# Attention heads beside an H3 convolution on one core: named jobs run from one list, PSUM as four pairs of banks

## The chip, the core and the metric

The kernel runs on one core of a Trainium2 chip. The metric is the device time of one execution in microseconds (us): the median of three runs. A profiled execution of the same program gives a trace, whose span runs from the first to the last instruction.

TensorE (PE in the profile) multiplies matrices and writes its results to PSUM, which is eight banks of 128 partitions x 512 float32 here. ScalarE (ACT) moves results from PSUM to the on-chip memory (an "evacuation" below) and makes exponentials, logarithms and sines. VectorE (DVE) makes the elementwise products and sums. GpSimd (POOL) and SyncE (SP) issue most of the DMA transfers. Each engine runs its own instructions in the order in which the program lists them; semaphores make one engine wait for another.

## What is computed

Two independent parts, both on a sequence of S = 2048 rows of D = 576, their outputs side by side in one array of 2048 x 1152 in bfloat16:

```python
# A: attention, 32 heads of 18; a row sees itself and 7 rows before it, 2 apart
qkv = x @ wqkv
logits[h, s, w] = (q[h, s] . k[h, s - 2w]) * 18 ** -0.5      # w = 0..7, masked where s - 2w < 0
a = (sum over w of softmax(logits)[h, s, w] * v[h, s - 2w]) @ wo
# B: H3
kv = (4-tap causal filter of k along the sequence, by shift_k) * v
y  = causal convolution of kv with ssm_k (length 2048), by FFT, + kv * ssm_D
b  = q * y
out = concat([a, b], -1)
```

## The kernel before

All weights and activations stay on the chip; the sequence is cut into two halves for A (1024 rows each) and four blocks of 512 rows for B. The work has these stages, with the lines of the kernel before:

- **Projection** (`project`, matmuls L363 and L367, tails L374 and L380, evacuation L397): for each component, half and tile of 128 channels, four k-tiles of 128 rows by 512 columns, plus a "tail" of 64 rows for the fifth k-tile. A flag decides whether the tails come first or last in a group. `transpose_tail` (L469) makes the input of the tails. `table_i` (L432) makes tables of sines for the inverse transform by transposing on TensorE and copying on ScalarE.
- **Shift filter** (`taps`, L554 to L580) on VectorE: four taps and the product with v, for each of the four blocks.
- **Spectra.** `mirror` (L589, L592) folds a block of kv and `fold_filter` (L650, L653) a block of the filter; `filter_spectrum` (L610, L611, L670) and `x_spectrum` (L766, L768) multiply by tables of sines and cosines. Each of these units is small: four to eight matmuls into one pair of banks, then one or two evacuations. `turn_filter`, `third`, `first_rows` and `negate` are small copies and sums around them, some as accumulating DMAs from POOL's queue.
- **Logits** (`logits`): VectorE multiplies q by shifted k (L822), TensorE sums over the channels of a head by a matrix of ones and zeros (L837), ScalarE evacuates (L842). Two half-passes (hh = 0 and 1) of ten products each.
- **Softmax** (`softmax`, L855 to L882): maxima and differences on VectorE (L865 to L869), the exponential on ScalarE (L871), the sum on TensorE (L877), the reciprocal by logarithm and exponential on ScalarE (L878, L879), the scaling on VectorE (L882).
- **Weighted values.** `spread` (L917) copies the probabilities of 32 heads' rows over the channels by four DMAs on SP's queue (L925); `weigh` multiplies by shifted v on VectorE (L947) and adds up on TensorE (L964, L978); ScalarE evacuates (L968, L982). There are six spreads, numbered 0 to 5, three for each half-pass.
- **Output projection** (`output`, L1012, L1020, L1031, stores L1035) with the weight that POOL's queue loads (L995, L998).
- **Convolution.** For each block j of the output, third t of the frequencies and block i of the input: a product of spectra on VectorE (L1098) and a sum on TensorE (L1126, evacuated at L1139, the last one by VectorE at L1137). Some products need the sum of two of a spectrum's three parts first (L1247). Then `inverse` (L1146; L1158, L1177, evacuated at L1161 and L1179), `back` (L1193; L1199, L1185, evacuated at L1206), and the gate by q on VectorE (L1212; the last block's in pieces at L1167). `load_q` (L1085) brings a block of q on POOL's queue into one of two slots; `store_b` (L1077) stores a gated block from the same slot, on SP's queue and partly on ScalarE's.

**What sets the order.** The program is written out by Python when it is built. VectorE's chain of logits, softmax and weighted values is the backbone, and small units of TensorE work wait in a queue `units`. At 48 places of the backbone `until` (L333) takes as many units from the queue as a hand-written tuple `PLACES` says; each time the first unit whose "due" time on a planner's clock has come. `dve` (L312) and `pe` (L318) advance these clocks by estimated durations; `need` (L340) takes units until none of a given name is left. Further tuples (`FKS`, `FXS`, `EARLY`, `AT`) place units in the queue.

**PSUM.** The eight banks are four pairs. A pool with two buffers has two tags, A and B, each of two pairs. Which tag a unit uses is fixed by its kind: projections, mirrors, folds and, until the logits run, filter spectra use A; logits, softmax sums, weighted values and spectral sums use B. Three kinds of small units pick among A and B by a turn of their own:

```python
    def filler_tag(kind, tags):
        turns[kind] += 1
        return tags[turns[kind] % len(tags)]
    def bank2(name, tag):
        return pp.tile([128, 2, 512], FP32, name=name, tag=tag)
```

A new tile of a tag waits until the tile two before it of the same tag has been evacuated.

Of the kernel before, what the change touches and what calls it, by code (L numbers as in the profile page):

```python
# [12 lines left out]
ALU = mybir.AluOpType  # L13
# [5 lines left out]
PLACES = (  # L19
    15, 4, 11, 2, 1, 0, 3, 4, 6, 4, 13, 4, 4, 0, 4, 3, 4, 2, 1, 3, 4, 3, 5, 5, 0, 7, 2, 2, 2, 1, 2, 2, 2, 2, 3,  # L20
    1, 0, 3, 2, 0, 8, 3, 0, 1, 12, 1, 1, 0,
)

FKS = (
    3, 1, 0, 0, 0, 0, 0, 0, 0, 0, 0, 0, 0, 0, 0, 0, 0, 0, 1, 0, 0, 0, 0, 2, 0, 0, 2, 0, 0, 0,
)
FXS = (
    7, 2, 0, 12, 13, 2, 0, 0, 4,
)

EARLY = (
    0, 0, 4,
)

AT = (
    2, 10, 17,
)
# [8 lines left out]
def kernel(  # L46
# [48 lines left out]
    pp = ctx.enter_context(tc.tile_pool(name="pp", bufs=2, space=PSUM))  # L95

    turns = {"fk": 0, "fx": 0, "wo": 0}

    def filler_tag(kind, tags):

        turns[kind] += 1
        return tags[turns[kind] % len(tags)]

    def bank2(name, tag):
        return pp.tile([128, 2, 512], FP32, name=name, tag=tag)

# [41 lines left out]
    warm = sp1.tile([128, 1], FP32, name="warm")  # L152
# [7 lines left out]
    def idle_work(n):  # L160
        ps = bank2("ps_idle", "A")
        for _ in range(n):
            nc.tensor.matmul(ps[:, 0, :], zeros[:, 0:128], zeros, start=True, stop=True)

# [137 lines left out]
    v = None  # L302
# [3 lines left out]

    units = deque()
    tasks = deque()
    clk = {"D": 0.0, "P": 0.0, "A": 0.0}
    psum = {"A": deque([0.0, 0.0]), "B": deque([0.0, 0.0])}  # L310

    def dve(n, fn, ready=0.0, ns=0.53):  # L312

        fn()
        clk["D"] = max(clk["D"], ready) + n * ns / 1000 + 0.125
        return clk["D"]

    def pe(us, tag, evac, ready=0.0, first=True, last=True):  # L318

        clk["P"] = max(clk["P"], ready, psum[tag].popleft() if first else 0.0) + us  # L320
        clk["A"] = max(clk["A"], clk["P"] + 0.1) + evac
        if last:
            psum[tag].append(clk["A"])
        return clk["A"]

    def pop(n=0):
        f = units[n][1]
        del units[n]
        f()

    places = iter(PLACES)

    def until():  # L333

        for _ in range(next(places, 0)):
            if units:
                p = max(clk["P"], psum["A"][0] if psum["A"] else 0.0)
                pop(next((n for n, u in enumerate(units) if len(u) < 4 or u[3] <= p), 0))

    def need(label):  # L340
        while any(u[2] == label for u in units):
            pop()

    def due(slack=0.0):

        while tasks and tasks[0][0] <= clk["D"] + slack:
            tasks.popleft()[1]()
# [4 lines left out]
    def dest(comp, ct):  # L352
        if comp == 0:
            return q, (ct * S if ct < 4 else 4 * S), 0
        return (k if comp == 1 else v), (ct * KW if ct < 4 else 4 * KW), PAD


    def project(comp, jj):
# [24 lines left out]
        def unit(ct, jj, jp, first, box):  # L383
            t, o, pad = dest(comp, ct)
            if jp == 0:
                box["ps"] = bank2("ps_proj", "A")
                if first:
                    tails(box["ps"], ct, jj, True)
            ps = box["ps"]
            body(ps, ct, jj, jp, first)  # L390
            if jp == 0:
                clk["P"] += 1.15 if first else 0.9
                return
            if not first:
                tails(ps, ct, jj, False)
            pe(0.9 if first else 1.15, "A", 1.02)
            nc.scalar.activation(view(t, o + pad + 1024 * jj, [[512, 2], [1, 512]]), ps[:], ACT.Copy)  # L397
            if ct == 4 and comp > 0:
                (nc.gpsimd if comp == 1 else nc.sync).dma_start(view(t, o, [[1, PAD]])[64:128, :], view(t, o + 1024, [[1, PAD]])[0:64, :])

        for ct in range(4) if jj < 2 else [4]:
            first = ct % 2 == 1 if ct < 4 else comp == 1
            box = {}
            for jp in range(2):
                units.append((0.9 + 0.25 * (jp != first), partial(unit, ct, jj % 2, jp, first, box),
                              f"v{jj}{ct}" if comp == 2 else f"proj{comp}"))
# [25 lines left out]
    def table_i(s):  # L432

        ps = bank2("ps_ti", "A")
# [6 lines left out]
        for g2 in range(2):  # L441
            nc.scalar.activation(view(TI, 1024 * s + 512 * g2, [[256, 2], [4, 64], [1, 4]]),
                                 view(ps, 512 * g2, [[256, 2], [1, 64], [64, 4]]), ACT.Copy)

# [17 lines left out]
    def pair_x():  # L462
        return pp.tile([128, 2, 1024], BF16, name="ps_x", tag="B")

    def early(f, us):
        f()
        clk["P"] += us

    def transpose_tail(jj):  # L469
        pt = pp.tile([128, 512], FP32, name="ps_x", tag="B")  # L470
# [4 lines left out]
        nc.scalar.activation(x5(jj), pt[:], ACT.Copy)  # L475

    def project_first(jp, ct0):

        ps = bank2("ps_proj", "A")
# [7 lines left out]
        nc.scalar.activation(view(q, S * ct0 + 512 * jp, [[S, 2], [1, 512]]), ps[:], ACT.Copy)  # L487

    def spread_taps(n0):
        n = min(256, D - n0)  # L490
        ps = bank2("ps_sk", "A" if n == 256 else "B")
        for h in range(0, n, 128):
            w = min(128, n - h)
            sk = skrow[:, 4 * (n0 + h):4 * (n0 + h + w)].rearrange("p (d j) -> p d j", j=4)
            for r in range(2):
# [4 lines left out]
                             ps[:].rearrange("p b (d j) -> p j (b d)", j=4)[:, :, 0:n], ACT.Copy)  # L500

# [3 lines left out]
    pts = [pair_x() for _ in range(2)]  # L505
# [6 lines left out]
    copy_tail(0, pts[1])  # L512
    spread_taps(256)
    sines += [table_x(0), table_x(1)]
    project_first(0, 0)
    pts = [pair_x() for _ in range(2)]
# [5 lines left out]
    copy_tail(1, pts[0])  # L522
    project_first(0, 2)
# [4 lines left out]
    for jj in range(2):  # L528
        if jj:
            project(0, jj)  # L530
# [773 lines left out]
```

## Time and profile before

| | |
|---|---|
| three runs | 213.05, 213.20, 213.38 us |
| median | 213.2 us |
| span of the profiled execution | 211.5 us |
| mean granted TensorE clock | 0.998 |
| busy: TensorE, VectorE | 200.9 and 197.3 us |
| busy: ScalarE, GpSimd | 151.0 and 69.3 us |
| moved by DMA | 36.12 MB, mean 171 GB/s |

In the rows below, a windows row has the stretch, its length, then for each engine (PE, PEld for weight loads, DVE, ACT, POOL) its busy time with the number of instructions, then the granted clock, the DMA share and GB/s. A waits row has the engine, the output and line that waited, the releaser it waited for, the total, the number of times and the longest, in us. A timeline row has the start, the length of the run of like instructions, the engine, the line, the operation with output and input, the number of them, and in brackets the idle time before it with what ended it. SPq is the issue of a DMA on SP's queue. A row of a group of instructions has their busy time and mean in ns, and then the idle time before them. A row of DMA issues ends in the median time from issue to landing.

### The profile page before, as it was taken

Reading aid. Unit: us, or ns where it says so; the run is one execution under the profiler, and the core shown is the slowest. Engines: PE = TensorE matmul, PEld = TensorE weight load, DVE = VectorE, ACT = ScalarE, POOL = GpSimd, SP = SyncE. Lnnn points to the kernel's source line nnn. Section 1 sums busy time; section 2 is a strip of 40 time slices with the busy share of each in tenths; the row PEclk is TensorE's granted clock in tenths of the full one; section 3 lists DMA queues with packets and bytes.
Section 4 is the critical chain, followed back from the end, with each engine's and each line's share of the span. In section 5 each row is a group of like instructions: output and inputs, shape, how many; then the busy total and the mean of one; then the engine's idle time right before and its main releaser. Section 6 shows DMA issues by size and latency. Waiting matters only on the chain.

```text
span 211.5 us, 5096 instructions
## 1 busy us (share of the span) xinstructions
PE 200.9 (95%) x2122; PEld 112.5 (53%) x2122; DVE 197.3 (93%) x150; ACT 151.0 (71%) x218; POOL 69.3 (33%) x104
## 2 busy tenths in 40 slices
PE   7999899999879999999999999999999999999891
PEld 2543344445545556563345566765567667676560
DVE  7989999999978999979979999999999999899982
ACT  3799766967797989984378688864487896765640
POOL 8999991023391367220090000004240000202000
PEclk9999999999999999999999999999999999999999
DMA  6999999999092636998999896589993105453034
GB/s 204 297 317 239 248 323 322 183 238 286 8 135 33 87 56 105 187 159 187 226 222 228 141 232 154 103 211 249 209 278 107 60 3 160 123 167 115 3 106 117
DMA packets 34084, 36.12 MB, mean 171 GB/s; under 512 B 17459, under 2 KB 28847, under 8 KB 34062
## 3 DMA queue, kind: packets, MB, share of 16 engines
q1 hardware_dynamic: 26380, 23.11, 43.8%
q0 software_dynamic: 5216, 10.19, 24.8%
q10 hardware_dynamic: 2466, 2.51, 3.6%
q8 instruction: 16, 0.26, 0.5%
q14 instruction: 6, 0.05, 0.1%
HBM read 13.11 MB, written 4.72 MB: 84 GB/s over the span
## 4 chain that ended last, share of the span: by engine, by line
PE 78%; ACT 10%; issue 3%; SPq 2%; DVE 2%; DMA 2%; DVEq 0%; ACTq 0%
PE ps_proj L363 13%; PE ps_z L1126 9%; PE ps_wo L1020 8%; PE ps_acc L964 7%; PE ps_inv L1158 7%; PE ps_fx L766 7%; PE ps_log L837 4%; PE ps_proj L483 4%; PE ps_fk L610 3%; ACT Ks L670 3%; PE ps_proj L374 2%; DMA Ks<-Ks 2%; SPq L212 2%; PE ps_rev L650 1%; PE ps_sk L496 1%
## 5 line engine op out<-in xcount | busy, mean ns | idle before, releaser
L363 PE MATMUL ps_proj<-xw 128*128 128x512 bf16 x160 | 37.5, 380 | 0.5 <-ACT qk L397 0.5
L822 DVE TENSOR_TENSOR av<-qk 128x4096 bf16<-128x4096 bf16 (+1 forms) x16 | 31.5, 2017 | 1.9 <-ACT xw L592 1.9
L363 PEld LDWEIGHTS <-xw 128*128 128x128 bf16 x160 | 14.4, 98 | 20.1 <-issue 4.8
L1139 ACT ACTIVATE av<-ps_z 128x768 bf16<-128x768 f32 x23 | 17.5, 811 | 5.6 <-PE ps_z L1126 5.6
L768 ACT ACTIVATE xw<-ps_fx 128x576 bf16<-128x576 f32 x32 | 18.8, 673 | 2.4 <-PE ps_fx L766 2.4
L397 ACT ACTIVATE qk<-ps_proj 128x1024 bf16<-128x1024 f32 x14 | 14.3, 1025 | 8.3 <-PE ps_proj L374 4.7
L670 ACT ACTIVATE Ks<-ps_fk 128x576 bf16<-128x576 f32 x32 | 19.0, 688 | 1.1 <-PE ps_fk L611 1.0
L1098 DVE TENSOR_TENSOR qk<-xw,Ks 128x2304 bf16<-128x2304 bf16 x14 | 18.6, 1355 | 1.0 <-PE ps_z L1126 0.7
L560 DVE TENSOR_TENSOR tB<-kj,skb 128x4608 bf16<-128x4608 bf16 (+1 forms) x8 | 19.3, 2416 | 0.1
L766 PE MATMUL ps_fx<-xw,TB 128*128 128x288 bf16 x128 | 17.9, 286 | 0.8 <-ACT xw L592 0.7
L1020 PE MATMUL ps_wo<-qk 128*128 128x288 bf16 x128 | 17.9, 287 | 0.0
L610 PE MATMUL ps_fk<-Ks,TB 128*128 128x384 bf16 x62 | 16.4, 326 | 1.2 <-ACT Ks L670 0.9
L1158 PE MATMUL ps_inv<-av,TI 128*128 128x288 bf16 (+1 forms) x112 | 15.6, 292 | 0.6 <-ACT av L1139 0.6
L766 PEld LDWEIGHTS <-TB 128*128 128x128 bf16 x128 | 12.0, 98 | 6.7 <-issue 3.5
L964 PE MATMUL ps_acc<-av,ident 64*64 64x512 bf16 x160 | 15.3, 379 | 0.0
L611 PE MATMUL ps_fk<-Ks,TB 128*128 128x192 bf16 x62 | 15.2, 246 | 0.0
L1087 POOL DMA_DIRECT2D TB<-in_B_q_dram x4 | 3.0, 738 | 36.7 <-DVE v L1098 23.5
L397 ACT ACTIVATE v<-ps_proj 128x1024 bf16<-128x1024 f32 x9 | 9.3, 1043 | 7.8 <-PE ps_proj L363 4.3
L1020 PEld LDWEIGHTS <-qk 128*128 128x128 bf16 x128 | 11.5, 98 | 6.2 <-issue 3.6
L968 ACT ACTIVATE qk<-ps_acc 128x1024 bf16<-128x1024 f32 x8 | 8.2, 1025 | 8.3 <-PE ps_acc L964 8.3
L947 DVE TENSOR_TENSOR av<-Ks,v 128x4096 bf16<-128x4096 bf16 x6 | 13.6, 2285 | 0.1
L1158 PEld LDWEIGHTS <-TI 128*128 128x128 bf16 x112 | 10.5, 98 | 5.6 <-issue 2.7
(194 smaller groups left out, 465.7 us busy)
## 6 DMA issues: line engine op xcount, KB each, us to landing
Ks<-Ks POOLq DMA_DIRECT2D x7, 576.0 KB, 8.3
TB<-av SPq DMA_DIRECT2D x12, 256.0 KB, 4.9
kj<-in_B_k_dram SPq DMA_DIRECT2D x6, 504.0 KB, 6.1
vt<-in_B_v_dram SPq DMA_DIRECT2D x8, 288.0 KB, 5.0
Ks<-av SPq DMA_DIRECT2D x8, 256.0 KB, 6.0
out_dram<-qk ACTq DMA_DIRECT2D x5, 288.0 KB, 3.2
Ks<-in_A_x_dram SPq DMA_DIRECT2D x2, 576.0 KB, 5.2
xw<-in_A_wqkv_dram SPq DMA_DIRECT2D x2, 576.0 KB, 6.0
```

The lines of the kernel that those rows point to most:

```text
L363: nc.tensor.matmul(ps[:, jp, :], wq(kb, comp, 128 * ct, 128), xT(kb, 1024 * jj + 512 * jp, 512), **se)
L397: nc.scalar.activation(view(t, o + pad + 1024 * jj, [[512, 2], [1, 512]]), ps[:], ACT.Copy)
L560: dve(2304 * n, lambda: nc.vector.tensor_tensor(to, view(kj, row * D, [[D, n], [D, 4], [1, D]]), view(skb, row * D, [[D, n], [0, 4], [1, D ...
L610: nc.tensor.matmul(o[:, 0:2], w, rhs[:, 0:2], start=start, stop=stop)
L670: nc.scalar.activation(view(Ks, k_at(m, cs ^ (m & 1)) + 96 * gi, [[768, 3], [384, 2], [1, 96]]), acc3(ps), ACT.Copy, scale=(PSG, MSG)[cs][ ...
L766: nc.tensor.matmul(ps[:, pm, 0:HD], TX[:, 2 * pm + c, 128 * gi:128 * gi + 128], kv[:, 2 * c + pm, HD * h:HD * h + HD], start=(c == 0), sto ...
L768: nc.scalar.activation(view(xw, HB * XG[i] + 96 * gi + 1152 * h, [[HB, 2], [384, 3], [1, 96]]), view(ps, 0, [[512, 2], [96, 3], [1, 96]]), ...
L822: return P, at, step, dve(1024 * nj, lambda: nc.vector.tensor_tensor(view(P, at, [[step, 4], [256, nj], [1, 256]]), view(t, o + 256 * hh, ...
L964: nc.tensor.matmul(acc[64 * o:64 * o + 64, h, :], ident[64 * h:64 * h + 64, 64 * h:64 * h + 64], view(P, 256 * u, [[2048, 2], [1, 256]])[6 ...
L1020: nc.tensor.matmul(ps[:, r, 0:HD], oT(hh, j + 2 * r, t)[:, o:o + 128], wo[:, t // 2, t % 2, HD * h:HD * h + HD], start=(t == 0 and h == 0) ...
L1126: nc.tensor.matmul(view(acc[r], 512 * h, [[192, 2], [96, 2], [1, 96]])[o:o + 64], w[64 * h:64 * h + 64, 64 * h:64 * h + 64], pr[64 * h:64 ...
L1158: nc.tensor.matmul(ps[:, c, 0:n], TI[:, sl, pm, 128 * c:128 * c + 128], Yall[:, j % 2, pm, sl, c0:c0 + n], start=(pm == 0 and sl == 0), st ...
```

## The change

The planner goes (`units`, `tasks`, `clk`, `psum`, `dve`, `pe`, `pop`, `until`, `need`, `PLACES` and the other tuples). Every piece of work becomes a function of its own with a name in a dictionary, and the program is written by running the names in the order of one string:

```diff
-PLACES = (
-    15, 4, 11, 2, 1, 0, 3, 4, 6, 4, 13, 4, 4, 0, 4, 3, 4, 2, 1, 3, 4, 3, 5, 5, 0, 7, 2, 2, 2, 1, 2, 2, 2, 2, 3,
...
+ORDER = """
+    k01a' k03a' k03b S1 Ex k00a' k00b I1 T0 Lk2 k02a' k02b k01b T1 Lv2 Lf0 Lo0 X5 k24a T2 k24b k10a M00 q24a
+    q24b Lk3 k10b Lf2 N2 M10 Lf1 Lv3 T3 k13a q10a' q11a' q10b k13b Lw RG0 Lf3 k11a' N3 k11b q12a q12b M01 Fr
+    q11b Lo1 SV q13a' L000 M11 k12a' k12b q13b x000 Lo2 N0 F2 x030 Z2 x031 K210 x021 Lo3 N1 F1 K213 M30 F3 K212
+    RG1 K200 x001 K203 L001 L002 F0 v00a' v00b K312 G000 L003 K112 M21 G001 G002 L004 L010 K310 x020 K211 K302
...
+    v02b G101 G102 K100 M31 U3 L104 G103 L110 K000 sm0c sm0d G104 L111 v01a' G110 v01b D1 v03a v03b x230 G111
+    L112 L113 G112 L114 K111 D0 Wl D2 x221 v11a' v11b V11 G113 G114 U2 x211 v12a v12b V10 sm1a sm1b v13a' v13b
+    V04 A10 V13 v10a' U1 sm1c A04 V12 v10b x310 x301 x321 x311 sm1d D3 x220 D4 A11 V20 x320 x231 x200 V21 x201
+    x210 V22 A20 V23 x011 x120 x130 x111 x131 x101 ak00 V34 A21 V40 D5 x331 V41 x300 O000 O001 A34 V42 x330 A40
...
+    i101 i02881 p211 b00 z220 p221 z210 z211 p222 z212 ak30 p301 z221 z222 b0288 ax30 g0 O131' i22880 i200
+    i12880 i201 Q2 i12881 p300 z300 p302 p303 z301 z302 z303 p311 b1288 i22881 p310 p312 p313 b10 z310 g1 z311
+    b2288 p320 p321 b20 z312 p322 z313 p323 O121' i300 z320 z321 i301 g2 z322 z323 b30 i3384L Q3 g30 g3384
+"""
...
+    jobs = {}
...
+    def job(name, fn, *args):
+        assert name not in jobs
+        jobs[name] = partial(fn, *args)
...
+    for name in ORDER.split():
+        jobs.pop(name.rstrip("'"))(*([True] if name[-1] == "'" else []))
```

The names: `kJCa` and `kJCb` (also q, v) are the two steps of a projection of half J (2: the tile shared by both halves) and channel tile C; a quote puts its tails first. `T` taps, `M` mirror, `F` fold, `K` filter spectrum, `x` input spectrum, `N` negate, `U` turn_filter, `Lk Lv Lf Lo Lw Wl Qj` loads and copies, `RG` reordering of the v weights, `Fr` first_rows, `I` table_i, `S1` the last sine, `Ex` the load of the exponential's table, `X5` transpose_tail, `SV` the opening of the second buffers. `Lhuc` and `Ghuc` are a logits product and its sum, `sm0a` to `sm1d` the softmax's four parts (differences, exponential, sum and reciprocal, scaling), `Dn` a spread, `Vnc` a weighted product, `Anc` its sum, `O` an output projection, `pjti` and `zjti` a product of spectra and its sum, `ak` and `ax` the sums of two parts, `i`, `b`, `g` inverse, back and gate.

Every tile of PSUM now comes from one queue of four pairs. A pair returns to its end when the program has listed its last evacuation:

```diff
-        return pp.tile([128, 2, 512], FP32, name=name, tag=tag)
...
+    slots = deque(range(4))
+    def banks(name, dtype=FP32):
+        n = slots.popleft()
+        return pp.tile([128, 2, 2048 // (4 if dtype == FP32 else 2)], dtype, name=name, tag=f"p{n}"), n
```

A unit, taking the projection and a filter spectrum as examples, changes so:

```diff
             if jp == 0:
-                box["ps"] = bank2("ps_proj", "A")
+                box["ps"], box["n"] = banks("ps_proj")
...
-            pe(0.9 if first else 1.15, "A", 1.02)
             nc.scalar.activation(view(t, o + pad + 1024 * jj, [[512, 2], [1, 512]]), ps[:], ACT.Copy)
+            slots.append(box["n"])
...
-            tag = filler_tag("fk", "AAB") if logits_run[0] else "A"
-            ps = bank2("ps_fk", tag)
...
+        ps, slot = banks("ps_fk")
```

The spreads' four DMAs, the matmuls, the activations and the products are the same instructions as before. The places in the on-chip memory that products of a kind use in turn are now given by four tuples (`LHOMES`, `VHOMES`, `OHOMES`, `PHOMES`). The sums of two parts for `ak0` and `ax0` keep their three pieces; the start of the program, up to the first four projections, keeps its order.

More of the change, by code (lines that the diff above doesn't have):

```diff
@@ L301 @@
     q, k = qk[:, 0:4 * S + 1024], qk[:, 4 * S + 1024:]
[L302 to L347, printed above, removed]
+    late = {}
     def halves(ap):
@@ L512 @@
     copy_tail(0, pts[1])
+    slots.extend(held)
     spread_taps(256)
@@ L515 @@
     project_first(0, 0)
-    pts = [pair_x() for _ in range(2)]
+    pts, held = zip(*[banks("ps_x", BF16) for _ in range(2)])
     for n in range(2):
```

861 lines of the change are left out of this document (359 added, 502 removed).

## The prediction

> **What bounds the kernel now.** I read the page's busy shares and the chain of waits first, then the windows, to see where the two busiest engines are idle.
>
> ```profile
> span 211.5 us, 5096 instructions
> PE 200.9 (95%) x2122; PEld 112.5 (53%) x2122; DVE 197.3 (93%) x150; ACT 151.0 (71%) x218; POOL 69.3 (33%) x104
> PE 78%; ACT 10%; issue 3%; SPq 2%; DVE 2%; DMA 2%; DVEq 0%; ACTq 0%
> ```
>
> ```profile
> 0.00:10.00 10.00, 8.70 (x44) 3.95 (x44) 8.55 (x21) 5.37 (x8) 8.94 (x23) 1.00 0.85 246
> ...
> 20.00:30.00 10.00, 9.45 (x79) 3.96 (x78) 9.85 (x6) 7.86 (x11) 9.76 (x14) 1.00 0.92 238
> ...
> 50.00:60.00 10.00, 8.80 (x84) 5.25 (x81) 9.90 (x9) 8.06 (x14) 5.04 (x8) 1.00 0.43 108
> 60.00:70.00 10.00, 9.04 (x96) 5.29 (x99) 8.14 (x7) 8.03 (x15) 5.55 (x8) 1.00 0.57 76
> ...
> 200.00:212.00 12.00, 6.79 (x112) 4.33 (x104) 6.55 (x8) 3.29 (x5) 0.00 (x0) 0.94 0.35 98
> ```
>
> TensorE is idle for 211.5 - 200.9 = 10.6 us: 1.3 at the start, 0.55 in 20 to 30, 1.20 + 0.96 = 2.16 in 50 to 70, 4.7 in the tail (11.5 - 6.79), and 1.9 in all other windows together. VectorE is idle 14.2 us. Both engines are nearly full, so each needs its own sum, and the later one sets the end. VectorE's waits name what it lacked:
>
> ```profile
> DVE av L822 <- ACT xw L592: 1.9, 1, 1.9
> ...
> DVE av L882 <- ACT av L879: 1.3, 1, 1.3
> DVE av L947 <- PE ps_log L837: 1.1, 1, 1.1
> DVE av L1137 <- PE ps_z L1126: 0.9, 1, 0.9
> ```
>
> ```profile
> 55.09 4.47 DVE L822 TENSOR_TENSOR av<-qk 128x4096 bf16<-128x4096 bf16 x2
> 142.53 2.29 DVE L947 TENSOR_TENSOR qk<-TB,v 128x4096 bf16<-128x4096 bf16 x1 [0.33 <-DMA TB<-av]
> 181.14 1.36 DVE L1098 TENSOR_TENSOR qk<-xw,Ks 128x2304 bf16<-128x2304 bf16 x1 [0.71 <-PE ps_z L1126]
> 201.88 1.35 DVE L1212 TENSOR_TENSOR TB<-v,TB 128x2304 bf16<-128x2304 bf16 x1
> 207.21 1.02 DVE L1167 TENSOR_TENSOR TB<-ps_back,TB 128x384 bf16<-128x384 f32 x2 [0.78 <-PE ps_back L1185]
> ```
>
> I wrote VectorE's 150 instructions of both kernels in program order, each at the start-to-start interval of its kind where it waits for nothing (2.20 us for a 4096-wide product, 1.27 for a 2304-wide one). Both lists sum to 196.3. An instruction's place in the list is its position; its start minus its position is VectorE's delay. The first logits product has position 51.8 and starts at 55.09, delay 3.3. The last full gate has position 191.7 and starts at 201.88, delay 10.2. Five waits make 1.85 + 1.30 + 1.12 + 0.33 + 0.71 = 5.3 of the rise (1.9 in the table is 1.85 in the timeline); the other 1.6 are small gaps. The two waits of the tail (0.91 and 0.78) and 3.3 us from the last product's end to the store's end complete it: 196.3 + 10.2 + 1.7 + 3.3 = 211.5.
>
> **The work itself.** Both programs have the same instructions on every engine (2122 matmuls, 150 on VectorE, 216 activations, 141 DMAs). Nothing is removed; only order, waits and PSUM homes move. A list read out at build time costs nothing on the chip. One thing differs by count: matmuls of different tile shapes stand side by side in 132 places instead of 130.
>
> ```profile
> 36.08 0.39 PE L374 MATMUL ps_proj<-xw 64*128 64x512 bf16 x2
> 36.40 3.63 PE L363 MATMUL ps_proj<-xw 128*128 128x512 bf16 x16
> 39.96 0.39 PE L374 MATMUL ps_proj<-xw 64*128 64x512 bf16 x2
> ```
>
> Sixteen full matmuls take 39.96 - 36.40 = 3.56 us, so about 0.216 each with one change of shape of 0.1 in the sum; the two half-height ones, which run side by side, take 0.32, again 0.1 more than one matmul. Two more changes cost +0.2 us. The Trainium skill, "TensorEngine Tiling (Array Packing)", section "Key Properties", says that changing the tiling mode drains TensorE; these rows agree, and were it not so the term would be 0.
>
> **PSUM as four pairs: the stage from 50 to 70.** Before, mirrors, folds and spectra share the two pairs of tag A, while B stands free.
>
> ```profile
> 56.16 0.41 PE L650 MATMUL ps_rev<-Ks,flip 128*128 128x288 bf16 x2 [0.68 <-ACT Ks L653]
> 60.22 0.32 PE L610 MATMUL ps_fk<-Ks,TB 128*128 128x384 bf16 x1 [0.74 <-ACT Ks L670]
> 62.76 0.65 PE L766 MATMUL ps_fx<-xw,TB 128*128 128x288 bf16 x4 [0.74 <-ACT xw L592]
> 57.33 1.19 ACT L653 ACTIVATE Ks<-ps_rev 128x576 bf16<-128x576 f32 x2 [0.68 <-PE ps_rev L650]
> L670 ACT ACTIVATE Ks<-ps_fk 128x576 bf16<-128x576 f32 x32 | 19.0, 688 | 1.1 <-PE ps_fk L611 1.0
> ```
>
> Each of the three waits is for an evacuation: a small unit takes some 0.5 us on TensorE (two 384- and two 192-wide matmuls) and up to 0.69 on ScalarE. The stage is ScalarE's by rate, so four pairs buy only depth: two more units in flight, 2 x 0.5 = 1.0 us. The new order strews the four folds among nine spectra there (F2, x030, x031, K210, x021 and on), so a backlog still builds: 9 x 0.19 = 1.7 us against 1.0 of cover, leaving about 0.7. Bounds are 0 (all covered) and 2.16 (the same waits elsewhere); I take 0.6, nearer the cover, since a projection (2 us on TensorE, 1.0 on ScalarE) follows. The gain is 1.5.
>
> **The early list.** The tails of the fifth k-tile (X5, k24) now stand behind a table load, the last sine and two table transposes on ScalarE. The old kernel's wait at that kind of place is
>
> ```profile
> 24.00 1.89 PE L363 MATMUL ps_proj<-xw 128*128 128x512 bf16 x8 [0.55 <-ACT qk L397]
> ```
>
> I take +0.3 net: between 0 and one evacuation more, 1.0. VectorE is full until 60, so this reaches the end through TensorE alone.
>
> **What VectorE then waits for.** In turn, counted as delay:
> - First product that needs a log sum's bank read: its position goes from 58.9 to 62.2, its matmuls' from 55.0 to 59.9 in TensorE's list. The room falls from 3.9 to 2.3 while TensorE is about 1.5 earlier. 1.85 becomes 1.65 (0.9 to 2.6): the order gives back what the banks bring.
> - The scaling of softmax 0 (1.30): +1.1 (0 to 1.3), since its sum stands at about the same distance.
> - The wait on the logits' tail (1.12): +0.25, because the weighted product that meets it first now takes another home.
> - Spread D1, for V11. Four DMAs on SP's queue copy the probabilities once they are scaled.
>
> ```profile
> 93.74 1.23 DVE L882 TENSOR_TENSOR av<-av 128x2048 bf16<-128x2048 bf16 x1 [1.30 <-ACT av L879]
> 95.03 2.99 SPq L925 DMA_DIRECT2D TB<-av  x4
> 118.66 1.22 DVE L882 TENSOR_TENSOR av<-av,xw 128x2048 bf16<-128x2048 bf16 x1
> 123.26 4.44 SPq L925 DMA_DIRECT2D Ks<-av  x4
> Ks<-av SPq DMA_DIRECT2D x8, 256.0 KB, 6.0
> TB<-av SPq DMA_DIRECT2D x12, 256.0 KB, 4.9
> ```
>
> Scaling ends at 94.9; the last of the first four issues goes out at about 97.4 to 98.0 and lands 4.9 to 6.0 later, so some 8.0 after the scaling. V11 stands 7.7 behind it in the new list (V01, the first, 11.1 in the old one). Wait 0.35 (0 to 3: a landing as slow as the next four, whose last ends 12 after the scaling, would be 4; only part of it is queueing).
> - Spread D4, for V40. Second on the queue behind D3: the scaling ends at 119.9, the last issue begins near 126.4 and lands near 132.5, 12.6 later. The new list gives it 11.5 (the old 13.2): +1.2 (0 to 2).
> - D5's 0.33 goes: V40's wait gives it more room. The 0.71 at 181.14 goes, with p301's bank read well ahead.
>
> Delay at the end: 3.3 + 1.65 + 1.1 + 0.25 + 0.35 + 1.2 = 7.85, and of the 1.6 of small gaps those 0.65 outside these places: 8.5, against 10.2.
>
> **The queues that carry the tail.** Block 3 of q goes into the slot that gate 1 has stored from, by POOL's queue:
>
> ```profile
> 185.11 1.35 DVE L1212 TENSOR_TENSOR TB<-v,TB 128x2304 bf16<-128x2304 bf16 x1
> 189.98 0.72 POOL L1087 DMA_DIRECT2D TB<-in_B_q_dram x1 [8.38 <-DMA out_dram<-TB]
> 190.70 1.20 POOL L1089 DMA_DIRECT2D TB<-in_B_q_dram x2
> TB<-in_B_q_dram POOLq DMA_DIRECT2D x8, 144.0 KB, 4.3
> ```
>
> Gate 1 ends at 186.46, the load goes out 3.5 later, its third issue near 191.3, and it lands 4.3 after that, near 195.3: 8.8 us after the gate (8.4 to 9.1). Hidden before, since the last gates come at 205. In the new list gate 1 moves from position 175.1 to 185.3, so it ends near 185.3 + 8.5 + 1.35 = 195.1 and q lands near 203.9. The full last product would be free at 194.3 + 8.5 = 202.8. So 1.1 of wait replaces the tail's 1.7. In the Trainium skill, "DMA: Bandwidth & Descriptors", section "Anatomy of one DMA — SWDGE (gpsimd) path", a semaphore wait is served on the issuing sequencer before dispatch; POOL's 8.38 us row agrees, and by that rule whatever stands behind a waiting load would be late too. Behind q's last load nothing stands; ahead of it in the new order, block 1 of q (Q1) stands before the third's load (Tk2), with 6 us of room by the positions.
>
> **The two sums.** VectorE: 196.3 + 8.5 + 1.1 + 3.3 = 209.2. TensorE: 211.5 + 0.2 + 0.3 - 1.5, less 0.5 of the 1.9 in the middle (VectorE's lateness that it shared), less 0.6 of the tail, where an output projection (O121) now stands ahead of the inverse that waited for an evacuation: 209.4. The later is 209.4. The profiled execution spans 211.5 and the median of the runs is 213.2, 1.7 more, which I add: 211.1 us.
>
> **The rivals.**
> A. The spreads come late and VectorE becomes the bound by its DMA waits. Place: V11 and V40. D1 lands 1.2 later and D3 with D4 2.5 later than taken, as they would if the weight load for the output (Wl) and D0, now issued around D1, shared the engines. VectorE: 209.2 + 3.7 = 212.9, time 214.6. It decides against the change from 2.5 us of extra wait (213.6). For it: 4.9 is a median, and issue of four already stretches from 2.99 to 4.44. Against: in the old profile only one such wait exists, 0.33.
> B. The change doesn't do what it says: ScalarE's rate, not the two pairs, sets the stage, and the waits move to the folds. TensorE: 211.5 + 0.2 + 0.3 - 0.5 = 211.5, time 213.2. For: 688 ns against 500. Against: ScalarE itself stands for 0.68 at 57.33 in that stage, for a fold that TensorE could not start, so depth counts.
> C. All is covered: stage 0.1, D1 and D4 in time. VectorE 209.2 - 1.55 = 207.65; TensorE 209.4 - 0.5 - 0.3 - 0.7 of the tail = 207.9; time 209.6.
> D. Gate 1's store or q's load takes 1.5 longer than the row: VectorE 210.7, time 212.4.
>
> **How the numbers follow.** Forecast 0.44, its own range 210.0 to 212.2. A 0.22, B 0.12, C 0.16, D 0.06. About 0.2% (0.4 us: 212.8 to 213.6) is what can be told from no change. Faster: forecast, C and D nearly whole, 0.65. Same: most of B and a little of A, 0.11. Slower: most of A and a rest of B, 0.24. The range runs from 208.0, C with the tail's 1.1 of wait and half of a microsecond of small gaps gone too, to 215.0, A at its price and the 0.4 that a measurement may add.
>
> **What would show it.** Right: TensorE's idle in 50 to 70 falls from 2.16 to under 1, no TensorE wait on L653 or L670's counterparts above 0.3; VectorE waits for DMA at V11 and V40 by 0.3 and 1.2; the delay at the last full gate is 8 to 9; the tail's last products wait for the load of q. Wrong: a VectorE wait on a DMA above 3 us (A); TensorE's idle unchanged with its waits still on ScalarE (B); a new wait on SP's or POOL's queue that this list doesn't name. A start-up stage that differs would upset all of it, as its code is unchanged.

## The result and the profile after

The changed kernel takes 226.2 us in the median of four runs (221.0, 224.3, 228.1 and 229.3), the kernel before 213.3 beside it. The ratio is 1.0443 (95% interval 1.0363 to 1.0523); like the ratios below it leaves out the longer runs, here those of 228.1 and 229.3 us, in which TensorE had a lower granted clock (0.970 and 0.963 against 0.984). The profile shown here is of the run of 229.3 us; the same stops stand in other kernels' profiles, the first in d1 and the other two in x1, both below. The forecast was 211.1 us, faster, with a range of 208.0 to 215.0. The change made the kernel slower, and the time lies outside the range.

The page after, and the windows in which TensorE is idle or its clock is low; the columns are those of before:

```profile
span 227.6 us, 5080 instructions
PE 205.2 (90%) x2112; PEld 115.1 (51%) x2122; DVE 197.9 (87%) x150; ACT 151.0 (66%) x218; POOL 69.7 (31%) x104
```

```profile
50.00:60.00 10.00, 5.96 (x42) 3.83 (x40) 9.90 (x8) 5.99 (x10) 4.92 (x6) 1.00 0.71 123
60.00:70.00 10.00, 9.10 (x61) 5.87 (x63) 5.93 (x5) 7.34 (x13) 6.01 (x7) 0.83 0.63 94
...
140.00:150.00 10.00, 4.30 (x59) 2.42 (x58) 4.48 (x3) 3.17 (x6) 0.00 (x0) 0.78 0.86 203
150.00:160.00 10.00, 9.93 (x95) 5.60 (x95) 7.71 (x5) 3.28 (x5) 0.00 (x0) 0.70 0.32 125
...
180.00:190.00 10.00, 7.50 (x104) 5.50 (x96) 7.49 (x6) 6.44 (x10) 0.00 (x0) 0.83 0.11 37
```

VectorE is busy for 197.9 us (197.3 before): the work is the same, and 15.5 us of idle time came in (29.7 against 14.2). Three stops hold it: 50 to 70, 138 to 160, and 178 to 190. After each the column of the clock, 1.00 before, falls to 0.83, 0.70 and 0.83. The waits of the changed kernel name a transfer at the root of each stop:

```profile
DVE av L808 <- DMA Ks<-av: 6.4, 1, 6.4
DVE av L700 <- ACT v L353: 6.3, 1, 6.3
...
PE ps_rev L598 <- DMA Ks<-Ks: 4.8, 1, 4.8
...
ACT qk L889 <- DMA out_dram<-qk: 3.5, 2, 3.3
...
PE ps_z L964 <- ACT qk L889: 2.5, 1, 2.5
```

VectorE's 6.3 us for ScalarE stand behind TensorE's 4.8 us for a DMA: the evacuation that VectorE waits for is of a projection that TensorE makes behind the late fold. (L598 is the fold, L700 a logits product, L808 a weighted product, L889 the output's evacuation.) The timeline of the changed kernel around the first stop:

```profile
46.51 6.00 SPq L211 DMA_TRANSPOSE Ks<-in_B_ssm_k_dram  x1
52.62 6.47 SPq L578 DMA_DIRECT2D Ks<-Ks  x6
...
60.75 0.64 PE L598 MATMUL ps_rev<-Ks,flip2r 128*128 128x288 bf16 x2 [4.78 <-DMA Ks<-Ks]
72.22 3.43 DVE L700 TENSOR_TENSOR av<-qk 128x4096 bf16<-128x4096 bf16 x2 [6.29 <-ACT v L353]
```

In the kernel before, the same copies and the first fold that needs them:

```profile
49.72 8.94 SPq L627 DMA_DIRECT2D Ks<-Ks  x6
65.31 0.41 PE L650 MATMUL ps_rev<-Ks,flip2r 128*128 128x288 bf16 x2
```

The fold F1 needs the six row copies of `first_rows` (L578), each pair of which waits for the pair before. They stand on SP's queue behind the fourth transpose, so the first goes out at 52.62 and the last lands after 60. Before, the copies went out between 49.7 and 58.7, no earlier in effect, but the folds that need them came later, at 65.31; the new list asks for the first of them at 55.97. The second stop, from the same timeline:

```profile
109.58 1.25 POOL L857 DMA_DIRECT2D qk<-in_A_wo_dram  x2 [11.29 <-DVE av L700]
...
113.05 2.48 POOL L622 DMA_DIRECT2D Ks<-Ks  x2
...
126.62 1.19 POOL L622 DMA_DIRECT2D Ks<-Ks  x1 [11.09 <-DMA Ks<-Ks]
129.46 1.18 POOL L622 DMA_DIRECT2D Ks<-Ks  x1 [1.65 <-DMA Ks<-Ks]
125.79 2.92 SPq L789 DMA_DIRECT2D TB<-av  x4
128.75 8.42 SPq L789 DMA_DIRECT2D Ks<-av  x4
145.52 2.29 DVE L808 TENSOR_TENSOR av<-Ks,v 128x4096 bf16<-128x4096 bf16 x1 [6.41 <-DMA Ks<-av]
```

and in the kernel before:

```profile
86.68 1.20 POOL L689 DMA_DIRECT2D Ks<-Ks  x1 [3.51 <-ACT Ks L670]
91.13 1.19 POOL L689 DMA_DIRECT2D Ks<-Ks  x1 [3.25 <-ACT v L397]
...
108.70 2.53 POOL L689 DMA_DIRECT2D Ks<-Ks  x2
```

L622 (L689 before) is an accumulating DMA of `turn_filter`. U2's pair goes out at 113.05, behind the load of the output weight (L857), which itself had waited 11.29 us. U1 writes the places that U2 reads, so it starts when U2 has landed: at 126.62, after 11.09 us of waiting, and at 129.46, in the middle of the spreads D3 and D4. D4's four issues take 8.42 us where they took 4.44, and V40 waits 6.41.

The third stop begins on the same queue. The accumulating DMAs of the two thirds went out at 144.10 and 146.01 before; now they stand beside the output's stores:

```profile
168.89 1.27 POOL L622 DMA_DIRECT2D Ks<-Ks  x1
171.55 1.82 POOL L622 DMA_DIRECT2D xw<-xw  x1
175.06 0.38 ACTq L893 DMA_DIRECT2D out_dram<-qk  x1
182.43 0.65 ACT L889 ACTIVATE qk<-ps_wo 128x576 bf16<-128x576 f32 x1 [3.34 <-DMA out_dram<-qk]
183.13 0.49 PE L964 MATMUL ps_z<-qk,identn 64*64 64x384 bf16 x4 [2.50 <-ACT qk L889]
```

### The profile page after: what moved, and what is told of

Its sections match the earlier page's. It is cut to its first block, busy times and chain, and to the rows that moved or that the text cites. A ratio compares the mean times of both kernels' runs of the same rounds, so it can differ in the third digit from the quotient of the medians.

```text
span 227.6 us, 5080 instructions
## 1 busy us (share of the span) xinstructions
PE 205.2 (90%) x2112; PEld 115.1 (51%) x2122; DVE 197.9 (87%) x150; ACT 151.0 (66%) x218; POOL 69.7 (31%) x104
## 4 chain that ended last, share of the span: by engine, by line
PE 26%; DVE 26%; DMA 24%; SPq 9%; issue 9%; ACT 2%; POOL 1%; DVEq 0%; POOLq 0%; ACTq 0%
DVE tB L513 6%; DVE xw L516 5%; SPq L789 5%; DMA out_dram<-qk 5%; DVE av L700 5%; DMA Ks<-av 4%; PE ps_z L964 4%; PE ps_wo L883 4%; DMA Ks<-Ks 3%; DMA TB<-av 3%; PE ps_acc L819 3%; PE ps_fk L563 3%; SPq L211 3%; PE ps_log L714 3%; DMA TB<-in_B_q_dram 2%
## 5 line engine op out<-in xcount | busy, mean ns | idle before, releaser
L320 PE MATMUL ps_proj<-xw 128*128 128x512 bf16 x151 | 37.0, 380 | 1.0 <-issue 0.8
L700 DVE TENSOR_TENSOR av<-qk 128x4096 bf16<-128x4096 bf16 (+1 forms) x16 | 31.8, 2017 | 6.6 <-ACT v L353 6.3
L819 PE MATMUL ps_acc<-av,ident 64*64 64x512 bf16 x160 | 17.2, 403 | 5.8 <-DVE av L808 5.8
L808 DVE TENSOR_TENSOR av<-Ks,v 128x4096 bf16<-128x4096 bf16 x6 | 13.6, 2288 | 7.5 <-DMA Ks<-av 6.4
L622 POOL DMA_DIRECT2D Ks<-Ks x7 | 8.6, 1296 | 35.3 <-ACT Ks L614 22.6
L883 PE MATMUL ps_wo<-qk 128*128 128x288 bf16 x128 | 19.1, 297 | 0.0
L563 PE MATMUL ps_fk<-Ks,TB 128*128 128x384 bf16 x62 | 17.1, 334 | 0.0
L819 PEld LDWEIGHTS <-ident 64*64 64x64 bf16 x256 | 8.2, 113 | 14.8 <-issue 5.4
L883 PEld LDWEIGHTS <-qk 128*128 128x128 bf16 x128 | 12.1, 101 | 6.1 <-issue 2.6
```

What stands on the lines that cost most here:

```text
L320: nc.tensor.matmul(ps[:, jp, :], wq(kb, comp, 128 * ct, 128), xT(kb, 1024 * jj + 512 * jp, 512), **se)
L563: nc.tensor.matmul(o[:, 0:2], w, rhs[:, 0:2], start=start, stop=stop)
L700: tt(view(P, at, [[step, 4], [256, nj], [1, 256]]), view(t, o + 256 * hh, [[0, 4], [512, nj], [1, 256]]), view(tk, ok + 2 + 8 * ug + 256 * ...
L819: nc.tensor.matmul(acc[64 * o:64 * o + 64, h, :], ident[64 * h:64 * h + 64, 64 * h:64 * h + 64], view(P[s], 256 * u, [[2048, 2], [1, 256]] ...
L883: nc.tensor.matmul(ps[:, r, 0:HD], oT(hh, j + 2 * r, t)[:, o:o + 128], wo[:, t // 2, t % 2, HD * h:HD * h + HD], start=(t == 0 and not fli ...
```

## The experiments

Sixteen runs of fifteen kernels, each beside the kernel before on the same chip. Medians are over all runs of a kernel. Several of these kernels scatter by some us from run to run; why is not shown. Where an effect is only a few us, the ratios are the safer comparison.

| kernel | median us | lowest to highest | ratio to before (95%) |
|---|---|---|---|
| e0, old order, four pairs | 210.4 | 210.2 to 211.1 | 0.9876 (0.9853 to 0.9900) |
| g0, the same again | 210.1 | 210.0 to 210.6 | 0.9875 (0.9860 to 0.9889) |
| g1, e0 with late turns | 215.6 | 214.8 to 217.5 | 1.0157 (1.0105 to 1.0208) |
| e1, F1 later | 229.1 | 227.6 to 231.4 | 1.0716 (1.0662 to 1.0770) |
| e2, turns ahead of Wl | 225.6 | 222.0 to 230.4 | 1.0485 (1.0399 to 1.0572) |
| e4, both and a store buffer | 228.7 | 228.3 to 229.2 | 1.0730 (1.0703 to 1.0757) |
| e6, folds spread, U1 named last | 230.0 | 228.9 to 230.4 | 1.0772 (1.0740 to 1.0805) |
| x1, no fold transfers | 224.8 | 220.3 to 225.5 | - |
| x2, no late turns | 218.7 | 212.7 to 221.1 | 1.0008 (0.9977 to 1.0039) |
| x3, none of them | 209.8 | 208.7 to 211.0 | 0.9830 (0.9779 to 0.9882) |
| d1, x3 with the row chain | 214.6 | 211.6 to 216.3 | 1.0007 (0.9965 to 1.0049) |
| d2, x3 with the folds' transfers | 210.2 | 209.1 to 211.0 | 0.9842 (0.9810 to 0.9874) |
| d3, x3 with the thirds' | 214.7 | 211.0 to 216.4 | 0.9999 (0.9958 to 1.0039) |
| d4, e0 with more VectorE work | 218.8 | 218.5 to 219.4 | 1.0268 (1.0244 to 1.0292) |
| f1, row chain on POOL's queue | 226.7 | 225.6 to 227.1 | 1.0624 (1.0586 to 1.0662) |
| f2, and turns and thirds moved | 227.8 | 225.9 to 228.9 | 1.0678 (1.0621 to 1.0736) |

**e0: PSUM alone.** The kernel before with its own order; a fixed list of 200 numbers gives each PSUM tile one of four pairs.

```diff
-        return pp.tile([128, 2, 512], FP32, name=name, tag=tag)
+        return pp.tile([128, 2, 512], FP32, name=name, tag=f"p{next(homes_ps)}")
```

> The kernel before with its own order on every engine; only PSUM changes: its 200 tiles take the four pairs of banks from one queue in the order of the program. Theory (the loss is in the new order, where transfers meet): four pairs cost nothing, the three waits of TensorE for ScalarE between 50 and 70 us (2.2 us together) shrink to under 1, and the time is 211.0 to 213.3 us. Rival 1 (one queue of pairs makes unrelated units wait for each other): new waits of TensorE on evacuations in the stages that had tag B to themselves, time above 216 us.

210.4 us, 1.2% under the kernel before and a little better than expected. Its windows in the stage of the small units:

```profile
50.00:60.00 10.00, 9.84 (x96) 6.21 (x92) 9.90 (x9) 8.96 (x15) 5.24 (x9) 1.00 0.55 131
60.00:70.00 10.00, 9.63 (x100) 5.23 (x97) 10.00 (x7) 8.72 (x16) 5.95 (x8) 1.00 0.79 105
```

TensorE's idle falls from 2.16 to 0.16 + 0.37 = 0.53. VectorE gains too: its first wait (1.85) is gone and the one at the scaling (1.30) is 0.65. Rival 1 is out: the loss is not in PSUM, and the change holds a gain that can be had without its order. It is the fastest kernel here that computes everything.

**e1, e2, e4: three edits of the new list.** e1 moves F1; e2 moves U2 and U1 ahead of the output weight; e4 does both and gives one output block the third store buffer. In e4 that buffer overlaps a place of the spectral products, so that one block of the output isn't the reference's.

```diff
-... Lo3 N1 F1 K213 M30 F3 ... L001 L002 F0 v00a' ...
+... Lo3 N1 K213 M30 F3 ... L001 L002 F1 F0 v00a' ...
-... L114 K111 D0 Wl D2 x221 ... G114 U2 x211 ... v10a' U1 sm1c ...
+... L114 K111 U2 U1 D0 Wl D2 x221 ... G114 x211 ... v10a' sm1c ...
```

> The changed kernel with one fold (F1) moved down to stand next to F0, so that the chain of six row copies on SP's queue has landed when TensorE comes to it. Theory: the 4.8 us wait of TensorE at the fold and the lower clock behind it (0.83 for 60 to 70 us) go, and VectorE's 6.3 us wait at its products with it: 4 to 6 us less than the changed kernel in the median, so 220 to 222 us, with the late stalls still there. Rival 1: nothing changes, 226 us. Rival 2 (the lower clock comes by itself and the waits follow from it): clock at 60 to 70 us is still below 0.9.

> The changed kernel with the accumulating DMAs of turn_filter (U2, U1) put on POOL's queue ahead of the load of the output weight (Wl), instead of behind it and beside the spreads D3 and D4. Theory: D4 lands within 13 us of the scaling instead of 20, V40's wait falls from 6.4 to under 2, TensorE's idle in 140 to 150 from 5.7 to under 1, and the clock of 0.78 and 0.70 behind it stays at 1: 6 to 9 us less, 217 to 220 us. Rival 3 (the spreads are late by themselves, by SP's queue): V40's wait stays above 5 us and the time at 224 to 228.

> The changed kernel with both moves above and a third: the output block that waits for its store (O130) takes the third store buffer. Theory: all three stalls go, no lower clock is left before the tail, 211 to 214 us, spread of the runs under 1 us. Rival 1: above 220 us. Rival 2: lower clock and a spread of several us stay.

None came down as expected. In e1 the fold's wait went, and others took its place: TensorE stands 1.80 us for a fold's accumulating DMA, and 3.89 for ScalarE, which itself waits 4.76 for one, for the folds now stand side by side and so do their DMAs on POOL's queue (three issues each from 63.89, 65.71 and 67.53). In e2 D4's wait shrank to 1.18, but D3 now waits 5.50: with U1 at 117 to 126 us the turns met D2 and D3 instead, and the load of the output weight, behind them on the queue, went out beside D3 (125.10 to 129); which of the two holds D3 up is not separated. e4 has the same wait at D3, 5.65. None of these moves removes a stop; each moves it.

**x1, x2, x3: transfers left out.** To see what the order costs without them, the accumulating DMAs are left out by kind, with four of the six row copies.

```diff
-        for step in range(3):                      # first_rows (x1, x3)
+        for step in range(1):
-        nc.gpsimd.dma_start(..., accum_op=ALU.add) # the three behind a fold (x1, x3)
-    for part in range(2):                          # turn_filter (x2, x3)
+    for part in range(2 if m == 3 else 0):
-        add_half(t, at + 2 * HB, at + HB)          # third (x3)
```

> The changed kernel without the accumulating DMAs behind each fold and with two instead of six row copies in first_rows, so the filter part of the output is not the reference's. Theory (TensorE's stop in 55 to 61 us is the latency of these transfers, which the new order meets too soon): TensorE waits less than 1 us in all between 50 and 80, VectorE has no wait over 2.5 us there, clock 1.00 in 60 to 70; the time is 5 to 7 us less than the changed kernel, 217 to 222 us, with D4's wait still there. Rival (moving F1 did not help because the stage is ScalarE's): VectorE's wait stays above 4 us.

> The changed kernel without the four accumulating DMAs of U2 and U1, so the filter's spectra of two blocks lack a term. Theory (D4 lands late because these four, 8 to 11 us each, share the DMA engines with the spreads): D3 and D4 take under 9 us to issue together instead of 11.3, V40 waits 0.3 to 2 us instead of 6.4, clock 1.00 in 140 to 160; 5 to 9 us less than the changed kernel, 217 to 221 us. Rival 3 (the spreads are late by themselves): V40 waits over 5 us.

> The changed kernel without the transfers left out in the two kernels above and without the accumulating DMAs of the two thirds (Tk2, Tx2). Theory: what is left is the order and PSUM alone, as the prediction took them: 208 to 213 us, clock above 0.99. Rival 4 (the order has waits of its own between engines beside the transfers): above 216 us.

x1 loses the first stop (TensorE has no wait for a DMA before 100 us) and keeps the second, 5.91 at V40. But its median of 224.8 is above the 217 to 222 expected, and its runs lie between 220.3 and 225.5, so x1 doesn't tell what the first stop costs; d1 below does. x2 keeps the first (9.31 on VectorE in the profiled run) and loses the second: D4's issues take 4.80 us. x3 loses all; its windows for the same stretches:

```profile
50.00:60.00 10.00, 9.95 (x77) 6.88 (x75) 9.90 (x8) 9.03 (x17) 1.84 (x3) 1.00 0.67 97
60.00:70.00 10.00, 10.00 (x89) 5.62 (x87) 9.60 (x8) 8.71 (x16) 0.00 (x0) 1.00 0.00 0
...
140.00:150.00 10.00, 10.00 (x123) 5.90 (x120) 10.00 (x7) 5.87 (x10) 0.00 (x0) 1.00 0.39 150
```

209.8 us: rival 4 is out. The order's own waits between engines are small: behind 50 us VectorE waits 3.8 us in all, against 7.0 in the kernel before. But beside e0, which has every transfer, the order gains nothing that can be told apart: the ratios are 0.9830 (0.9779 to 0.9882) and 0.9876 (0.9853 to 0.9900).

**e6: an order against the stops.**

```diff
-... F1 K213 M30 F3 K212 RG1 K200 x001 K203 L001 L002 F0 v00a' v00b K312 G000 ... L010 K310 ... U1 sm1c ... V40 D5
+... K213 M30 F3 K212 RG1 x001 K203 L001 L002 F1 v00a' v00b K200 K312 G000 ... L010 F0 K310 ... sm1c ... V40 D5 U1
```

> The changed kernel, computing everything, with its two swapped folds a few microseconds apart and later (F1 behind L002, F0 behind L010), K200 later, and U1 behind D5. Theory: the stop in 50 to 65 us shrinks to under 3 us as no fold's transfers stand behind another's; U1 no longer meets D3 and D4, V40's wait under 3 us: 215 to 220 us. Rival 4: 224 us or more.

230.0 us. U1's place in the list hardly moved its DMAs: they go out at 129.06 and 132.31 (126.62 and 129.46 in the changed kernel).

```profile
129.06 1.19 POOL L622 DMA_DIRECT2D Ks<-Ks  x1 [10.39 <-DMA Ks<-Ks]
```

In both places U1 waits for U2's landing, with nothing between them on POOL's queue. A place in the list sets what an instruction stands behind on its own queue, not a time. V40's wait did fall to 2.44, but D3's rose to 2.35, and the first stop moved to the other fold: TensorE waits 4.02 there and VectorE 6.90 behind it.

**d1, d2, d3: one kind put back into x3 at a time.**

> The kernel that left out all three kinds of transfers (209.8 us), with the chain of six row copies (first_rows) put back alone; the accumulating DMAs of folds, turns and thirds stay out. Theory: the chain is the first thing that TensorE meets (in the changed kernel its last copy landed when the fold F1 had waited 4.8 us); the fold waits 3 to 5 us, VectorE 2 to 5 at its products, 212 to 215 us. Rival (the chain is late only because accumulating DMAs stand beside it): fold waits under 1 us, 209 to 211 us.

> The 209.8 us kernel with the accumulating DMAs of the four folds put back alone. Theory: they cost less than the row chain here, since the spectra that need them stand further back: 210 to 213 us, waits of TensorE and ScalarE on them under 3 us. Rival: they are the stop by themselves, 214 us or more.

> The 209.8 us kernel with the accumulating DMAs of the two thirds (Tk2, Tx2) put back alone. They stand behind the load of q on POOL's queue and so beside the output's stores. Theory: the stores land late, ScalarE waits 2 to 3 us for one of them and TensorE 2 us behind it, of which VectorE loses 2: 211 to 212.5 us. Rival: no wait, 209.8 us.

The row chain brings 4.8 us by the medians (fold's wait 3.30, VectorE's 5.02), the folds' own transfers 0.4, the thirds 4.9. By the ratios, times 213.2, they are 3.8, 0.3 and 3.6. The thirds cost more than expected. d3's profiled run is 3.7 us longer than x3's, and VectorE's waits behind 50 us account for that, 7.4 in all against 3.8: ScalarE waits 3.0 for a store, TensorE 2.2 behind it and VectorE 2.0 + 0.4 behind that; the rest is at two spreads and in the tail.

With the turns (226.2 - 218.7 = 7.5 by x2) the sum of the medians is 209.8 + 4.8 + 0.4 + 4.9 + 7.5 = 227.4, against 226.2 measured. That it comes so near is luck. By the ratios the turns are 9.3, and the four parts make 3.8 + 0.3 + 3.6 + 9.3 = 17.0, against 13.1 between x3 and the changed kernel. Three parts were put back alone and one was taken out, so they need not add up.

**g1: the late turns alone, in the old order.**

```diff
-            if (gi, cs) == (3, 0) and 0 < m < NBL - 1:
-                turn_filter(m + 1)
+            if (gi, cs) == (3, 0) and m == 2:
+                turn_filter(3)
...
+    turn_filter(2)
     turn_filter(1)
```

> The old order with four pairs (210.4 us), and one piece of the new order alone: the accumulating DMAs of U2 stand behind the output weight's load on POOL's queue, directly ahead of U1's, as in the changed kernel, instead of some 20 us earlier; nothing else moves. Theory (their place in time makes D4 late): U1 then meets D3 and D4, the issue of D3 and D4 stretches from 8 us to over 10, V40's counterpart waits 3 to 7 us, the clock falls behind it: 214 to 219 us. Rival (D4 is late in the changed kernel by another part of the order, such as D0 and Wl beside D1): 210 to 212 us.

> The old order with four pairs once more, on the same chip as the kernel above: 210.2 to 211.1 us, 1.0 to 1.5 per cent under the kernel before.

215.6 against 210.1 on the same chip. The spreads' issues of g0, and then g1's with the turns (L698) and VectorE's two new waits:

```profile
117.23 3.30 SPq L934 DMA_DIRECT2D TB<-av  x4
120.63 4.10 SPq L934 DMA_DIRECT2D Ks<-av  x4
```

```profile
116.06 1.19 POOL L698 DMA_DIRECT2D Ks<-Ks  x1 [7.41 <-ACT xw L777]
118.65 1.18 POOL L698 DMA_DIRECT2D Ks<-Ks  x1 [1.41 <-DMA Ks<-Ks]
117.33 6.91 SPq L934 DMA_DIRECT2D TB<-av  x4
124.33 7.01 SPq L934 DMA_DIRECT2D Ks<-av  x4
131.03 2.29 DVE L956 TENSOR_TENSOR av<-TB,v 128x4096 bf16<-128x4096 bf16 x1 [2.65 <-DMA TB<-av]
135.39 2.29 DVE L956 TENSOR_TENSOR av<-Ks,v 128x4096 bf16<-128x4096 bf16 x1 [2.07 <-DMA Ks<-av]
```

Eight issues that took 7.4 us take 13.9. The edit moves U2 behind the weight's load, and U1 follows it later (116.06 instead of 106.02 in g0); nothing else was moved. So this is shown: two accumulating DMAs beside the spreads are enough to make them late. The two waits are 4.7 of the 4.8 us between the two spans. One part of the expectation failed. TensorE stands 3.0 us for VectorE and soon 1.6 more, and in this profile its clock stays at 1.00:

```profile
130.00:140.00 10.00, 5.39 (x74) 3.62 (x70) 6.90 (x4) 5.51 (x9) 0.00 (x0) 1.00 0.93 181
140.00:150.00 10.00, 10.00 (x134) 5.75 (x137) 10.00 (x5) 4.65 (x6) 2.36 (x2) 1.00 0.72 191
```

**d4: a stop without any transfer.** One weighted product is made four times, with the same result.

```diff
+            for _ in range(3 if (n, ct) == (4, 0) else 0):
+                nc.vector.tensor_tensor(...)       # the product that follows, once more
```

> The old order with four pairs (210.4 us) with one weighted product (the first of spread 4) made four times instead of once: 3 x 2.2 = 6.6 us more work on VectorE, at the place where the changed kernel stood for D4, and TensorE stands behind it for some 4 us. Theory (a stop of TensorE lowers its granted clock afterwards): clock under 0.9 in the 20 us after, time up by 6.6 plus 1 to 4 us, 218 to 221 us. Rival 2 (the lower clock has another cause): clock 1.00, 217.0 us.

```profile
130.00:140.00 10.00, 5.21 (x72) 3.57 (x64) 9.90 (x6) 5.54 (x10) 0.00 (x0) 1.00 0.77 164
140.00:150.00 10.00, 8.41 (x80) 4.12 (x84) 8.87 (x4) 2.33 (x3) 1.19 (x1) 0.66 0.45 104
```

TensorE stands 4.58 us for VectorE and 1.6 more shortly after, and then runs at 0.66 in the next window. The time rises by 8.4 to 8.7 us for 6.6 of work, and VectorE's two new waits for TensorE behind the stop, 1.10 and 0.83, are the difference. In the changed kernel the same pair of waits (1.10 and 1.19) stands behind V40. Here VectorE's added work made the stop, so the lower clock follows it and is not its cause.

**f1, f2: the whole computation, transfers moved.** f1 issues the row copies on POOL's queue behind the second transpose; f2 also holds U1's DMAs until a late product is made and puts the thirds' ahead of q's load.

```diff
-... N2 M10 Lf1 Lv3 T3 ... q12b M01 Fr q11b ...
+... N2 M10 Lf1 Fr Lv3 T3 ... q12b M01 q11b ...
-                nc.sync.dma_start(*((spare[m], row(m, 0)), ...
+                nc.gpsimd.dma_start(*((spare[m], row(m, 0)), ...
+    job("W1", lambda: nc.gpsimd.tensor_copy(scratch[:], weight_home(4, 3)[:, 0:1]))
-... v10a' U1 sm1c ... V43 O101 ... p000 z000 Q1 ... z101 Tk2 ... p201 Tx2 ...
+... v10a' sm1c ... V43 W1 U1 O101 ... Tk2 Tx2 p000 z000 Q1 ... z101 ... p201 ...
```

> The changed kernel, computing everything, with the six row copies issued from POOL's queue as soon as the two transposes that they read have landed, instead of from SP's queue behind the fourth transpose. Theory: the chain lands by 55 us, the fold F1 waits under 1 us, no clock below 0.95 in 55 to 70, VectorE has no wait over 2 us before the softmax; the late stops stay: 218 to 222 us. Rival (the fold waits for its transfers wherever they are issued, six copies in a row being slow in themselves): the wait stays at 4 us or more, 224 to 228 us.

> As the kernel above, and with two more moves: U1's accumulating DMAs are held on POOL's queue by a one-column copy that reads a late product of spread 4 (so that they start after D3 and D4 have landed), and the thirds' DMAs stand ahead of q's first load instead of behind it. Theory: D4's wait falls under 2 us, no store makes ScalarE wait over 1 us, clock above 0.99 before the tail: 210 to 214 us with a spread of the runs under 2 us. Rival 4 (U2's transfers alone fill the engines enough): D4's wait above 4 us, 216 us or more.

Neither came down. In f1 the fold no longer waits, but the copies hold POOL's queue until 55, and with it two plain copies (54.99 instead of 45.62); the first fold's own DMAs behind those go out five us later (60.17 instead of 55.08), and TensorE stands 3.55 for them. In f2 D4's wait is gone, and a store beside the moved DMAs takes its place: ScalarE waits 9.79 us for it, and VectorE behind that:

```profile
177.91 1.36 DVE L948 TENSOR_TENSOR qk<-xw,Ks 128x2304 bf16<-128x2304 bf16 x1 [9.69 <-PE ps_z L967]
```

## Why the prediction was wrong

**The sum came near only where the transfers were left out, and in part by luck.** 211.1 was forecast, and x3, the order and PSUM with most of the accumulating DMAs left out, takes 209.8. But the terms differ: the waits taken for VectorE ahead of the tail were 1.65 + 1.1 + 0.25 + 0.35 + 1.2 = 4.55 us, and x3 has 2.0; the tail's wait was taken as 1.1, and x3 has 1.8 (1.00 for ScalarE, 0.81 for q's load).

**The term for PSUM was right in mechanism.** 1.5 was forecast for the stage from 50 to 70; e0 saves 2.16 - 0.53 = 1.63 of TensorE's idle there. The whole gain, 2.6 to 2.7 by e0 and g0, is larger, since VectorE's first two waits go or shrink as well. The prediction held that the order gives the first of these back. Rival B, in which the pairs change nothing, is refuted.

**The first step that failed is the early list.** "VectorE is full until 60, so this reaches the end through TensorE alone", and the wait of the first product that needs a log sum's bank read as 1.65 us (0.9 to 2.6). It was 6.29. I compared positions in the lists of TensorE and VectorE and moved the folds forward with them, but did not follow what F1 reads: a chain of three dependent steps of tiny copies, which starts when the queue ahead of it is done. The trace of before had its end (its row copies were issued until 58.7), and the new list wants the fold at 56. d1 shows the chain alone: the fold waits 3.30 and VectorE 5.02. In the changed kernel TensorE's idle in 50 to 70 rose to 4.04 + 0.90 = 4.94, where under 1 was forecast. A step that is pulled forward does not bring its inputs' landing times with it.

**The second is the price of D4**, 1.2 (0 to 2). It measured 6.41. The price was worked out from where D4 is issued and from its landing in the old profile, which holds only while the same transfers stand around it. In the new list U2 stands behind the last spectrum of its block, K111, which is evacuated at 108.30, and behind the output weight's load; so U2 and U1 start at 113 and 126 us instead of U2 near 87 and U1 at 109. My list of moved DMAs spoke of Wl and D0, and left the turns out. g1 shows that the turns alone are enough. Rival A had the right place and sign (V40 by D4, and its mark of a wait above 3 us for a DMA), the wrong neighbours, and 2.5 us where 5.2 more came. D1, costed the same way at 0.35, measured 0.31. (A's limit is a slip of addition: 209.2 + 2.5 + 1.7 is 213.4, not 213.6; nothing hangs on it.)

**The third is POOL's queue at the end.** "Behind q's last load nothing stands; ahead of it ... block 1 of q (Q1) stands before the third's load (Tk2), with 6 us of room". The room was for the third's own user. The third then moves beside the output's stores, and one store holds up ScalarE for 3.34 us and TensorE behind it for 2.50. Here the rule cited from the Trainium skill, "DMA: Bandwidth & Descriptors", section "Anatomy of one DMA — SWDGE (gpsimd) path", that a wait is served on the issuing sequencer, was the one to follow further: f1 shows its cost (5 us for what stands behind the waiting copies).

**No term stood for the clock.** In the changed kernel, d1 and d4, stops of 2.5 to 4.8 us were followed by windows at 0.66 to 0.88. The Trainium skill, "TensorE: Matmul & The Clock Gate", section "HAM oscillation — how this bites in real kernels", warns of idle gaps over about 3.4 us; here 3.30 (d1) and 2.50 (below) were enough. But the 3.0 us in g1 and stops of 2.0 to 2.3 us in d2, d3 and x2 left the clock at 1.00, so the length of the stop alone does not decide it.

The tail was near: the last products wait 0.78 us for q's load in the changed kernel, against 1.1 forecast.

What stays open: whether the thirds alone make the stores late, since in d2, without the thirds' accumulating DMAs, ScalarE also waits 2.57 us for a store and VectorE 2.26 behind it, without x3 showing the like; why several kernels scatter by some us; and whether a place in this order exists where all transfers land in time. Six kernels that move transfers (e1, e2, e4, e6, f1, f2) moved the stops, and none removed them all.

## What to carry to other kernels

When an order is rewritten, list the transfers of both orders by the time at which they would start, big accumulating ones above all, and price every transfer by who runs beside it in the new order, not by its landing in the old profile. A change of buffers and a change of order are best tried apart: here the first alone is 1.2% faster and the second hides it. An engine's list sum is a lower bound; it is reached only if its inputs' chains, down to the smallest copies, are moved as early as the work that reads them.

## What the hardware showed

Two accumulating DMAs of 576 KB beside the eight of the spreads stretched the issue of these from 7.4 us (g0) to 13.9 (g1). A store of 288 KB, 3.2 us in the median of the old profile, took 7.3 us beside the thirds' (issued at 175.06, its buffer free at 182.4). A stop of TensorE can cost twice. Windows of 2 us of the changed kernel around the third one, a wait of 2.50 us that ends at 183.13:

```profile
180.00:182.00 2.00, 0.63 (x16) 0.31 (x9) 2.00 (x2) 0.00 (x0) 0.00 (x0) 1.00 0.53 172
182.00:184.00 2.00, 0.87 (x13) 0.57 (x16) 1.50 (x2) 1.57 (x3) 0.00 (x0) 0.81 0.03 13
184.00:186.00 2.00, 2.00 (x32) 1.56 (x28) 1.36 (x1) 1.77 (x4) 0.00 (x0) 0.50 0.00 0
186.00:188.00 2.00, 2.00 (x39) 1.48 (x32) 1.00 (x1) 1.44 (x3) 0.00 (x0) 0.84 0.00 0
```

The clock falls to 0.50 in the third row, and over the last three rows 2 x (0.19 + 0.50 + 0.16) = 1.7 us of TensorE are lost beside the 2.5. Over the whole span it is (1 - 0.963) x 227.6 = 8.4 us of the profiled run; part of it lies under VectorE's work.
